# A rank for every piece of a planned kernel, and the transfers of an untaken path moved to another engine

## The chip, the cores and the metric

The kernel runs on one core of a Trainium2 chip. A core has a matmul engine (TensorE, PE in the profile; its weight loads are PEld), VectorE (DVE), ScalarE (ACT), GpSimd (POOL) and SyncE (SP), which here only issues transfers (DMAs). On-chip data lie in SBUF (128 partitions); TensorE writes into PSUM, eight banks per partition. The metric is the device time of one execution in microseconds, the median of some runs. An execution taken with the profiler gives the trace; its span runs from the program's first to its last instruction and is a little shorter than its time.

## The reference

Two stages: a linear attention with decay over 4 batches, 8 heads, 768 steps and head dimension 48, and a feed-forward layer whose hidden value is the maximum of three products, on the 3072 resulting tokens.

```python
# r, k, v: (4, 8, 768, 48); w, u: (8, 48)
for t in range(S):
    cur = np.einsum('bhd,bhe->bhde', u[None] * kt, vt)
    y[:, :, t] = np.einsum('bhd,bhde->bhe', rt, state + cur)
    state = w[None, :, :, None] * state + np.einsum('bhd,bhe->bhde', kt, vt)
x = y.transpose(0, 2, 1, 3).reshape(B * S, H * D)          # (3072, 384)
h = np.maximum(np.maximum(x @ w1, x @ w2), x @ w3)         # (3072, 768)
out = h @ w_out                                            # (3072, 384)
```

All is float32; the kernel reaches that accuracy by splitting operands into a high and a low float16 part and adding three products.

## The kernel before

The 768 steps are cut into 12 chunks of 64. A chunk has two halves `q` of four heads each. For each half the attention makes scores (`sc`: keys against receptances, masked, with the `u` term on the diagonal, in `am`), values (`va`: the masked scores against the values plus the receptances against the state) and the state's update (`ke`). In chunks 0 and 1 this is done in float32; from chunk 2 on with parts in float16 (`kd`, `ktd`, `vd`, `sd`, `rh`/`rl`, `ah`/`al`; the high part is a ScalarE copy, the low part a VectorE subtraction: L444, L449, L451, L490, L601). From chunk 4 on the parts are first spread into block-diagonal tiles by transfers (`kb`, `ktb`, `vb`, `sb`), so that a matmul uses the whole 128x128 array (L538); before that the array is used in 64-wide corners (L541, L548). From chunk 3 on GpSimd does the elementwise multiplications (`scale` L480, `product` L499 and L500, `diagonal` L516, `decay` L522), before that VectorE.

The chunk's result becomes `x` (L667, L670; six small transfers put its last rows in place, L677). The feed-forward then makes, for six groups `f` and three weights, nine matmuls each (`up`, L693). ScalarE takes the first of the three products (L708), VectorE the maximum with the other two (L712), ScalarE the high part `hh` (L715), GpSimd the low part `hl` (L721; the last group's by VectorE). Then come the matmuls with the output weight (`down`, also L693), a ScalarE copy to `io` (L738) and the store (L1103). The eight weights come as 64-bit floats and are converted on ScalarE and VectorE during the first 80 us (L351, L355, L358, L361). `STIRS` = 22 groups of three matmuls on zeros (L689) fill TensorE's early gaps.

The order of all this is written out by a planner, `Plan`, when the program is made. Each piece of work is entered by a call of `do` with its due time, its engine, a cost in us, the function that emits its instructions, what it reads, writes and which buffer it takes. `order` then goes forward in modelled time: of the engine that can start first it takes, among the pieces that are ready, the one with the lowest `due`. All engines get their instructions in the resulting order; they then run on their own and wait for each other through semaphores. Before the change `due` is the caller's figure plus a shift from a table `SHIFT` by the piece's kind ("dve m", "pe sc") and its stage (five stages, bounded by the due times 0, 1, 2 and 10). A transfer's completion uses one of eight semaphores in turn, so that a transfer waits until the one eight places ahead of it has landed (in the planner: `LANES`).

At the end VectorE makes a flag that says whether all inputs lay in the range for which the fast path is exact; every engine loads it (L1149) and branches (L1159): if the flag is set, a general path (`general`) computes everything again, slowly, in float32. With these inputs the flag is not set, and each engine jumps over its part of that path. Its transfers are all issued by SP.

```python
            n = first(m for m in when if self.todo[m]["eng"] == self.ENGINES[e] and when[m] <= t + 0.02)
...
    with tc.If(got["go"] > 0):
        general()
```

Of the kernel before, what the change touches and what calls it, by code (L numbers as in the profile page):

```python
# [7 lines left out]
F32 = mybir.dt.float32  # L8
# [22 lines left out]
FEATURE = 2  # L31
HELPED = dict(scale=3, product=3, diagonal=3, decay=3)
# [41 lines left out]
class Plan:  # L74
# [6 lines left out]
    SHIFT = {  # L81
        "sp feat": (0.06, 2.41, 0.07, -2.37, 0),
        "sp tok": (4.64, -12.96, -5.22, 0.22, 0),
        "pe blank": (-0.35, 0, 0, 0, 0),
        "pool pad": (0, -0.41, -0.49, 0, 0),
        "dve kT": (0.95, 1.8, 0, 0, 0),
        "dve rT": (-2.97, 3.27, 0.98, 0, 0),
        "act ru": (-3.24, 2.09, 0, 0, 0),
        "pe bo": (-20.47, 6.44, 0, 0, 0),
        "dve am": (1.11, 102.24, -0.18, -0.19, 0.43),  # L90
        "pe sc": (-3.66, -0.77, -0.03, -0.83, -0.79),
        "pool vz": (-5.54, 0, 0, 0, 0),
        "act apart": (0.53, 0, 0, 0, 0),
        "pe va": (-1.26, 17.06, -22.44, -45.09, 3.03),
        "act xh": (-2.11, 6.29, 19.78, -2.05, -0.03),
        "dve xl": (-0.63, -5.4, -2.29, -1.83, 0.76),
        "act xsq": (0, -4.27, 17.76, -6.93, -1.42),
        "act u": (0, 1.78, 0, 0, 0),
        "dve tkf": (0, -7.35, 0, 0, 0),
        "pe turned": (0, -0.4, 0, 0, 0),  # L100
        "act tkt": (0, -2, 0, 0, 0),
        "pe stir": (0, 0.62, 1.56, 0.64, 1.31),
        "sp word": (3.62, 3.5, 0, 0, 0),
        "act ztop": (-5.52, -0.56, 0, 0, 0),
        "dve word": (2.04, 0, 0, 0, 0),
        "act his": (0.41, -4.8, 0, 0, 0),
        "dve lo": (1.13, -2.95, 0, 0, 0),
        "pe kp": (0.04, -16.13, 0, 0, 0),
        "act kt": (-0.4, -0.46, 0, 0, 0),
        "pe ke": (-10.27, -1.26, 0.08, 0, 0),  # L110
        "act state": (0, -0.83, 0, 0, 0),
        "act sq": (0, 0, -3.6, 6.45, -0.3),
        "act sd": (0, 14.27, 0, 0, 0),
        "dve state": (-1.48, -1.03, 1, -1.84, 0),
        "act sdh": (0, -0.64, 23.47, -0.59, 0),
        "dve sdl": (-4.22, 1.55, 7.23, -1.96, 0),
        "sp x3": (0, 2.95, -1.73, -0.89, 0.43),
        "pe up": (0, -3.62, 0.01, -0.2, -0.43),
        "act m": (-0.7, -4.9, 0, 1.38, -1.96),
        "dve m": (93.3, -556.17, 6.75, 0.9, 1.16),  # L120
        "act hh": (-2.49, -6.05, 2.12, -0.02, -11.37),
        "pool hl": (2.58, 5.89, 0.11, -4.17, 3.89),
        "dve hl": (0, -1.12, 1.62, 0, -0.03),
        "pe dn": (0, -1.32, -44.06, -0.15, 0.87),
        "act io": (0, -1.2, 1.65, -2.57, 0),
        "sp io": (0, -0.82, -6.31, -0.75, 2.37),
        "act kdh": (0, -1.05, -4.12, 0.03, 0.27),
        "dve kdl": (0, -5.77, 1.73, 1.56, 0),
        "act rh": (0, -2.11, 0, 2.07, 3.23),
        "dve rl": (0, 6.31, 0.65, 0.14, -1.72),  # L130
        "dve a": (0, -5.82, 10.67, 18.29, 0.93),
        "act am": (0, 0, 0.68, 0, 0),
        "act ah": (0, -2.27, 0, 24.09, -0.46),
        "dve al": (0, 1.56, -1.03, -0.22, -0.05),
        "dve kdec": (0, 3.63, -1, 0, 0),
        "act ktdh": (0, 8.15, -0.28, -1.81, 0),
        "dve ktdl": (0, -0.05, -0.41, -1.02, 0),
        "act vdh": (0, -0.74, 0, 2.92, -4.09),
# [117 lines left out]
def kernel(ctx, tc, feat, tok, wu, ut, ws, wo, cst, out):  # L256
# [208 lines left out]
    def units(a):  # L465
        return a.rearrange("p g b n -> p (g b) n")
# [753 lines left out]
```

## Time and profile before

| | us |
|---|---|
| runs | 384.31, 387.48, 384.63; median 384.63 |
| the profiled execution | 384.0 |
| its span | 382.1, at a granted TensorE clock of 0.998 |
| TensorE busy | 372.6 (98%) |
| VectorE, ScalarE, GpSimd busy | 253.9, 243.1, 188.9 |

Matmuls are pipelined and their ends are modelled: in a dense stretch a matmul starts 109 ns after the one before it, while its own row is 273 ns long. Busy time is the union of the rows, so a stall of TensorE shows as idle time only where it outlasts the row before it. In a stage's row stand the stretch's bounds and length, then busy us (and instruction counts) of PE, PEld, DVE, ACT and POOL, the granted clock, the transfers' share of the DMA engines and GB/s. In a wait's row stand the engine and line that waited, who released it, us in total, times, and the longest. A row of one source line has its instructions with minimum, median and maximum duration in ns and the first and last start in us; "SPq" and the like are the engine's sequencer, which branches, waits and issues transfers. The chain of waits follows back from the last instruction to what released each step.

### The profile page before, as it was taken

How to read it: one execution, taken by the hardware profiler on the slowest of the kernel's cores; microseconds unless marked ns; L12 is line 12 of the kernel's file. 1: busy time of each engine (PE TensorE's matmuls, PEld its weight loads, DVE VectorE, ACT ScalarE, POOL GpSimd, SP SyncE). 2: the span in 40 equal slices, each digit the busy share in tenths (PEclk: the TensorE clock that was granted, in tenths of full speed). 3: DMA queues.
4: the chain of work that ended last, by engine and by line, in shares of the span. 5: the costliest groups of instructions: out<-in, count | busy, mean ns of one | idle time of the engine just before them, and what ended most of it. 6: DMA issues, size and time to landing. Idle time of an engine off the chain costs nothing.

```text
span 382.1 us, 13571 instructions
## 1 busy us (share of the span) xinstructions
PE 372.6 (98%) x5660; PEld 335.1 (88%) x5660; DVE 253.9 (66%) x457; ACT 243.1 (64%) x623; POOL 188.9 (49%) x190
## 2 busy tenths in 40 slices
PE   8999999989999999999999999999999999999994
PEld 7899888878898999998998999999999999999883
DVE  5599999999868657558468667667757555122340
ACT  3899758778557637656647556656655935993611
POOL 8500333899995585456556557547736320020110
PEclk9999999999999999999999999999999999999999
DMA  8985737162996888959986996996986964731201
GB/s 294 359 294 201 296 122 238 52 237 67 277 269 139 259 237 225 277 150 267 275 243 160 272 264 172 270 264 176 276 230 181 233 164 112 247 105 34 81 2 50
DMA packets 27700, 77.13 MB, mean 202 GB/s; under 512 B 4784, under 2 KB 12272, under 8 KB 26608
## 3 DMA queue, kind: packets, MB, share of 16 engines
q1 hardware_dynamic: 27344, 75.96, 69.0%
q8 instruction: 46, 0.75, 0.9%
q10 hardware_dynamic: 288, 0.23, 0.2%
q14 instruction: 22, 0.18, 0.2%
HBM read 38.38 MB, written 4.72 MB: 113 GB/s over the span
## 4 chain that ended last, share of the span: by engine, by line
PE 82%; DVE 8%; ACT 3%; DMA 3%; issue 2%; POOL 0%; SPq 0%; ACTq 0%; DVEq 0%
PE psm L693 63%; PE psv L538 8%; PE psa L538 3%; PE psm L689 2%; DMA raw<-in_wo_dram 2%; PE psa L548 1%; DMA tok<-in_tok_dram 1%; PE psv L541 1%; ACT ztop L351 1%; DVE raw L355 1%; DVE m L712 1%; DVE kd L449 1%; PE psa L582 1%; DVE sd L451 1%; DVE vd L451 1%
## 5 line engine op out<-in xcount | busy, mean ns | idle before, releaser
L693 PEld LDWEIGHTS <-w 128*128 128x128 f16 x2592 | 249.0, 98 | 31.2 <-issue 2.3
L693 PE MATMUL psm<-x,w 128*128 128x256 f16 x1944 | 225.2, 273 | 1.0 <-DVE m L712 1.0
L721 POOL TENSOR_TENSOR hl<-m,hh 128x256 f16<-128x256 f32 x60 | 46.8, 780 | 124.9 <-ACT hh L715 124.9
L712 DVE SCALAR_TENSOR_TENSOR m<-psm,m 128x256 f32<-128x256 f32 x144 | 60.2, 418 | 59.3 <-PE psm L693 50.1
L715 ACT CAST hh<-m 128x256 f16<-128x256 f32 x72 | 28.9, 401 | 53.3 <-DVE m L712 53.0
L480 POOL TENSOR_TENSOR feat<-feat,wrt 128x512 f32<-128x512 f32 x36 | 51.6, 1453 | 19.8 <-DVE ktd L449 10.2
L693 PE MATMUL psm<-hh,w 128*128 128x256 f16 x432 | 55.9, 273 | 0.0
L463 ACT ACTIVATE junk<-tok 128x384 bf16<-128x384 f32 x72 | 37.3, 518 | 3.0 <-DMA tok<-in_tok_dram 2.1
L708 ACT ACTIVATE m<-psm 128x256 f32<-128x256 f32 x72 | 27.2, 378 | 16.1 <-PE psm L693 15.1
L693 PE MATMUL psm<-hl,w 128*128 128x256 f16 x216 | 33.4, 273 | 0.6 <-DVE hl L721 0.4
L499 POOL TENSOR_TENSOR am<-tok,u_sb 128x384 f32<-128x384 f32 x18 | 20.2, 1122 | 24.9 <-DVE al L601 20.8
L490 DVE TENSOR_TENSOR rl<-feat,rh 128x512 f16<-128x512 f32 x20 | 17.6, 879 | 11.4 <-ACT rh L485 11.4
L670 DVE SCALAR_TENSOR_TENSOR x<-psv,x 112x512 f16<-112x512 f32 (+2 forms) x24 | 16.1, 671 | 12.3 <-ACT x L667 12.3
L516 POOL TENSOR_TENSOR am<-cs,a 128x512 f32<-128x512 f32 x18 | 20.6, 1146 | 6.3 <-DVE a L507 6.1
L538 PE MATMUL psv<-rh,sb 128*128 128x64 f16 x256 | 23.6, 193 | 0.0
L538 PE MATMUL psv<-ah,vb 128*128 128x64 f16 x256 | 23.6, 193 | 0.0
L538 PE MATMUL psv<-al,vb 128*128 128x64 f16 x128 | 22.7, 193 | 0.0
L538 PE MATMUL psv<-rl,sb 128*128 128x64 f16 x128 | 22.7, 193 | 0.0
L538 PEld LDWEIGHTS <-vb 128*128 128x128 f16 x384 | 21.1, 98 | 0.4
L500 POOL TENSOR_TENSOR am<-am,tok 128x384 f32<-128x384 f32 x18 | 20.7, 1150 | 1.4
L738 ACT ACTIVATE io<-psm 128x256 f32<-128x256 f32 x36 | 13.0, 380 | 12.4 <-PE psm L693 12.0
L507 DVE TENSOR_REDUCE a<-am 128x8 f32<-128x384 f32 x20 | 11.0, 548 | 14.3 <-POOL am L500 14.2
(124 smaller groups left out, 582.6 us busy)
## 6 DMA issues: line engine op xcount, KB each, us to landing
tok<-in_tok_dram SPq DMA_DIRECT2D x26, 576.0 KB, 6.2
feat<-in_feat_dram SPq DMA_DIRECT2D x24, 512.0 KB, 4.7
raw<-in_ws_dram SPq DMA_DIRECT2D x6, 1152.0 KB, 7.8
out_dram<-io SPq DMA_DIRECT2D x36, 128.0 KB, 5.2
kb<-kd SPq DMA_DIRECT2D x16, 256.0 KB, 5.8
vb<-vd SPq DMA_DIRECT2D x16, 256.0 KB, 5.9
sb<-sd SPq DMA_DIRECT2D x16, 256.0 KB, 5.2
kb<-kd SPq DMA_DIRECT2D x16, 248.0 KB, 5.8
```

Of the source, the lines that this page charges most:

```text
L463: nc.scalar.activation(out=junk[:, 0:U * D].rearrange("p (u d) -> p u d", u=U), in_=src, func=AF.Square, scale=scale, accum_out=stat[:, ki ...
L480: helper(c, "scale").tensor_tensor(out=t[n], in0=t[n], in1=tb, op=ALU.mult)
L490: nc.vector.tensor_tensor(out=t["rl"], in0=units(t["rT"]), in1=t["rh"], op=ALU.subtract)
L499: helper(c, "product").tensor_tensor(out=w.rearrange("p (g b) d -> p g b d", g=2), in0=t["r"], in1=by_token(u_sb, q), op=ALU.mult)
L500: helper(c, "product").tensor_tensor(out=w, in0=w, in1=units(t["k"]), op=ALU.mult)
L516: helper(c, "diagonal").tensor_tensor(out=t["a"], in0=eye.unsqueeze(1).broadcast_to([P, U, C]), in1=t.pop("sum").unsqueeze(2).broadcast_to ...
L538: nc.tensor.matmul(out=ps[:, i, :], lhsT=block[k].on[a][i], rhs=prods[k](b, i), **flags)
L693: nc.tensor.matmul(out=ps, lhsT=a, rhs=b, start=first and n == 0, stop=last and n == len(prods) - 1)
L708: nc.scalar.mul(out=m, in_=ps, mul=by)
L712: nc.vector.scalar_tensor_tensor(out=m, in0=ps, scalar=by, in1=m, op0=ALU.mult, op1=ALU.max)
L715: nc.scalar.copy(out=h[0][:, f, :], in_=m)
L721: lows_by(c, f).tensor_tensor(out=h[1][:, f, :], in0=m, in1=h[0][:, f, :], op=ALU.subtract)
```

## The change

Three things are changed.

1. The table of shifts by kind and stage is replaced by `RANK`, 1593 whole numbers, one for each call of `do` in the order of the calls. A piece's number takes the place of its due time among the ready pieces. With it some of the planner's costs change: the small moves of `x` count 0.74 us each on SP and the spreads 0.58 (0.45 before); GpSimd's multiplications are 12% dearer in chunks before 6, its low parts 0.82 us instead of 0.70 in chunks before 5.
2. The transfers of the general path (`general`, and `load_weight` called from it) are issued by ScalarE instead of SP.
3. Five output stores (three of chunk 8, two of chunk 9) are issued as two halves of 128 columns each.

Beside these, the array of tokens holds r, k, v in this order instead of k, r, v, and there is a loader `load_kv` for chunks between `FLIPPED` and `FEATURE`, which are both 2.

```diff
 CORNERS = 4
 STIRS = 22
 FEATURE = 2
+FLIPPED = 2
 HELPED = dict(scale=3, product=3, diagonal=3, decay=3)
 SC_R = 2.0 ** 6
...
     ISSUE = {"sp": 0.45, "act": 0.45, "pool": 1.0}
     BEFORE, BEHIND, PHASE, LANES, TURN = 1.5, 1.0, 1.4, 8, 0.095
     CLASSES = (0.0, 1.0, 2.0, 10.0)
-    SHIFT = {
-        "sp feat": (0.06, 2.41, 0.07, -2.37, 0),
-        "sp tok": (4.64, -12.96, -5.22, 0.22, 0),
-        "pe blank": (-0.35, 0, 0, 0, 0),
...
-    }
+    RANK = (
+        10, 30, 47, 0, 64, 6, 688, 43, 378, 140, 582, 295, 115, 293, 348, 331, 608, 352, 377, 429, 127, 269, 239, 107,
+        112, 94, 226, 96, 102, 206, 244, 142, 89, 166, 63, 256, 65, 285, 93, 70, 213, 21, 932, 674, 186, 23, 18, 114,
...
+    )
     def __init__(self, bufs):
         self.bufs, self.todo, self.wrote, self.read = bufs, [], {}, {}
     def do(self, due, eng, cost, fn, reads=(), writes=(), takes=(), move=0, near=0, parts=1, counts=1.0, corner=False):
-
-
         n = len(self.todo)
         new = [t for _, t in takes]
         made = (*new, *writes, *reads)[0]
         kind = eng + " " + (made if isinstance(made, str) else made[0])
         stage = sum(due >= x for x in self.CLASSES)
         base = due
-        due += self.SHIFT.get(kind, (0,) * 5)[stage]
+        due = self.RANK[n]
         need = {self.wrote[k] for k in (*reads, *writes) if k in self.wrote}
         for k in writes:
             need |= self.read.get(k, set())
...
     def load_tok(c, q):
         t = raw.tile([P, 3, 2, B, D], F32, name="tok")
         nc.sync.dma_start(out=t, in_=tok[c, q])
-        raws.setdefault((c, q), {}).update(k=t[:, 0], r=t[:, 1], v=t[:, 2])
+        raws.setdefault((c, q), {}).update(r=t[:, 0], k=t[:, 1], v=t[:, 2])
         return t
+    def load_kv(c, q):
+        t = raw.tile([P, 3, 2, B, D], F32, name="tok")
+        nc.sync.dma_start(out=t[:, 1:], in_=tok[c, q][:, 1:])
+        raws.setdefault((c, q), {}).update(k=t[:, 1], v=t[:, 2])
+
     def load_v(c, q):
-        t = raw.tile([P, 2, B, D], F32, name="v1", bufs=4)
+        t = raw.tile([P, 2, B, D], F32, name="v1", bufs=2 * FLIPPED)
         nc.sync.dma_start(out=t, in_=tok[c, q][:, 2])
         raws.setdefault((c, q), {}).update(v=t)
...
     def by_down(t, f, ms):
         return t.rearrange("p (f n) -> p f n", f=3)[:, f % 3, ms]
-    def load_weight(n, h=None, shift=0):
+    def load_weight(n, h=None, shift=0, eng=nc.sync):
         raw = wld.tile([P, 4 * WN + 4], I16, name="raw64")
         src = (ws[n] if n < NF else wo[n - NF]).bitcast(I16)
         cols = slice(0, 4 * WN) if h is None else slice(h * 4 * HN, (h + 1) * 4 * HN)
-        nc.sync.dma_start(out=raw[:, shift:shift + cols.stop - cols.start], in_=src[:, cols])
+        eng.dma_start(out=raw[:, shift:shift + cols.stop - cols.start], in_=src[:, cols])
         return raw
...
-            rw = load_weight(n, h).bitcast(I32)[:, 0:2 * HN].rearrange("p (n two) -> p n two", two=2)
+            rw = load_weight(n, h, eng=nc.scalar).bitcast(I32)[:, 0:2 * HN].rearrange("p (n two) -> p n two", two=2)
...
-                nc.sync.dma_start(out=t.rearrange("p (q g) b s -> p q g b s", q=2), in_=feat[bass.ds(c, 1), :, :, i].rearrange("c q p g b s -> p (c q) g b s"))
+                nc.scalar.dma_start(out=t.rearrange("p (q g) b s -> p q g b s", q=2), in_=feat[bass.ds(c, 1), :, :, i].rearrange("c q p g b s -> p (c q) g b s"))
...
-                    nc.sync.dma_start(out=ov, in_=o.rearrange("p (i two s) -> p i two s", i=1, two=2))
+                    nc.scalar.dma_start(out=ov, in_=o.rearrange("p (i two s) -> p i two s", i=1, two=2))
...
-    def dma(due, fn, move, reads=(), writes=(), takes=(), eng="sp", n=1):
-        do(due, eng, n * Plan.ISSUE[eng], fn, reads, writes, takes, move, 0, n)
+    def dma(due, fn, move, reads=(), writes=(), takes=(), eng="sp", n=1, each=0.45):
+        do(due, eng, n * each, fn, reads, writes, takes, move, 0, n)
     def helping(c, columns, what):
-        return ("pool", 0.05 + 2.5e-3 * columns) if c >= HELPED[what] else ("dve", dve(columns))
+        return ("pool", (1.12 if c < 6 else 1.0) * (0.05 + 2.5e-3 * columns)) if c >= HELPED[what] else ("dve", dve(columns))
     def dve(columns):
         return 0.07 + 1.05e-3 * columns
...
     def fetched(c, q, due, behind=()):
         dma(due, lambda: load_feat(c, q), 1.8, reads=behind, writes=["fetched"], takes=[("feat", ("feat", c, q))])
+        if c < FLIPPED:
+            dma(due, lambda: load_v(c, q), 0.85, reads=behind, writes=["fetched"], takes=[("v1", ("tok", c, q))])
+            return
         if c < FEATURE:
-            dma(due, lambda: load_v(c, q), 0.85, reads=behind, writes=["fetched"], takes=[("v1", ("tok", c, q))])
+            dma(due, lambda: load_kv(c, q), 1.67, reads=behind, writes=["fetched"], takes=[("tok", ("tok", c, q))])
             return
         dma(due, lambda: load_tok(c, q), 2.5, reads=behind, writes=["fetched"], takes=[("tok", ("tok", c, q))])
     def late_squares(c, q, due):
         t = ("again", c, q)
         dma(due, lambda: do_tile(t, load_tok(c, q)), 2.5, reads=[("begun", int(due))], writes=["fetched"], takes=[("tok", t)])
-        for kind, n in enumerate((1, 0, 2)):
+        for kind, n in enumerate(range(3)):
             do(due + 0.2, "act", 0.62, lambda kind=kind, n=n: square_sum(units(T[t][:, n]), kind, c, q), reads=[t], writes=[("sq", c, q, "rkv"[kind])])
     def squares(c, q, due):
...
     def spreading(c, due, dst, src, keys, name):
         if c >= CORNERS:
-            dma(due, lambda: spread(nc.sync, dst, src), 2.4, reads=[*keys, *(("pad", n) for n in range(14))], writes=[name], n=2)
+            dma(due, lambda: spread(nc.sync, dst, src), 2.4, reads=[*keys, *(("pad", n) for n in range(14))], writes=[name], n=2, each=0.58)
...
         do(due + 0.04, "dve", 0.40 if half else 0.68, lambda: x_low(c, q, T["x", c]), reads=[("va", c, q), hi], writes=[lo])
         if not begins:
             if c:
-                dma(due + 0.06, lambda: x_last(T["x", c]), 0.4, reads=[hi, lo], writes=[rest], n=2 * NJ)
+                dma(due + 0.06, lambda: x_last(T["x", c]), 0.4, reads=[hi, lo], writes=[rest], n=2 * NJ, each=0.74)
             do(due + 0.9, "act", 0.97, lambda: x_sum(c, T["x", c]), reads=[hi, rest], writes=[("xsq", c)])
     def attend(c, at):
...
             m = ("m", c, f)
             do(due - 0.1, "act", act(TOK), hi, reads=[m, *([("hh", c)] if f else [])], writes=[("hh", c, f)], takes=[] if f else [("hh", ("hh", c))])
-            do(due - 0.1, *(("dve", dve(TOK)) if lows_by(c, f) is nc.vector else ("pool", 0.7)), lo, reads=[m, ("hh", c, f), *([("hl", c)] if f else [])],
+            do(due - 0.1, *(("dve", dve(TOK)) if lows_by(c, f) is nc.vector else ("pool", 0.82 if c < 5 else 0.7)), lo, reads=[m, ("hh", c, f), *([("hl", c)] if f else [])],
                writes=[("hl", c, f)], takes=[] if f else [("hl", ("hl", c))], near=0.55)
         banks = {}
...
             do(due, "pe", len(fs) * 0.328, lambda: down(T["h", c], m, fs, banks, TOK), reads=reads, **(dict(takes=[("psm", bank)]) if 0 in fs else dict(writes=[bank])))
             if NF - 1 in fs:
                 do(due + 0.02, "act", act(TOK), lambda: do_tile(("io", c, m), leaving(banks[m], TOK, SC_O)), reads=[bank], takes=[("io", ("io", c, m))])
-                dma(due + 0.03, lambda: nc.sync.dma_start(out=out[m, :, c * TOK:(c + 1) * TOK], in_=T["io", c, m]), 0.1, reads=[("io", c, m)])
+                ways = 2 if (NCH - 4) * NM <= c * NM + m < (NCH - 4) * NM + 5 else 1
+                dma(due + 0.03, lambda: stored(m, ways), 0.1, reads=[("io", c, m)], n=ways)
+
+        def stored(m, ways):
+            for k in range(0, TOK, TOK // ways):
+                nc.sync.dma_start(out=out[m, :, c * TOK + k:c * TOK + k + TOK // ways], in_=T["io", c, m][:, k:k + TOK // ways])
         most, rest = range(NF - 1), [NF - 1]
         for m, fs, due in ((0, most, 0.70), (1, most, 0.77), (0, rest, 0.83), (1, rest, 0.85), (2, range(NF), 0.87)):
...
     ws = ws.reshape(NF, P, 3 * DM)
     wo = words(inputs["moe_w_out"]).reshape(2, 3, P, DM).transpose(0, 2, 1, 3).reshape(2, P, 3 * DM)
     ft = np.stack([feat(inputs["k"]), feat(inputs["r"])], axis=3)
-    tk = np.stack([tokm(inputs["k"]), tokm(inputs["r"]), tokm(inputs["v"])], axis=3)
+    tk = np.stack([tokm(inputs["r"]), tokm(inputs["k"]), tokm(inputs["v"])], axis=3)
     wu = np.stack([feat1(inputs["w"]), feat1(inputs["u"])], axis=1)
     s, t = np.arange(P)[:, None] % C, np.arange(C)[None]
     cst = np.concatenate([np.eye(P), s == t, s < t, np.arange(P)[:, None] // C == np.arange(2)[None]], axis=1).astype(np.float32)
```

More of the change, by code (lines that the diff above doesn't have):

```diff
@@ L606, in keys @@
         if c < WHOLE:
-            whole(t["ke"], D, (t.pop("kt") if c < FEATURE else units(t["k"]), units(t["v"])))
+            whole(t["ke"], D, (t.pop("kt") if c < FLIPPED else units(t["k"]), units(t["v"])))
         else:
@@ L812, in general @@
                     row = tok[bass.ds(c, 1), :, hh * C + s:hh * C + s + 1, 2].rearrange("c q p g b e -> (c p) q g b e")
-                    nc.sync.dma_start(out=vr[HS[hh]].rearrange("p (q g) b e -> p q g b e", q=2), in_=row.broadcast_to([C, 2, 2, B, D]))
+                    nc.scalar.dma_start(out=vr[HS[hh]].rearrange("p (q g) b e -> p q g b e", q=2), in_=row.broadcast_to([C, 2, 2, B, D]))
                 kc, rc = (t[:, :, :, s:s + 1].broadcast_to([P, NP, B, D]) for t in cols)
@@ L833, in general @@
                     nc.scalar.copy(out=ys[:, q], in_=ps)
-                nc.sync.dma_start(out=y[bass.ds(c, 1), s].rearrange("c h g b e -> (c h) (g b e)"), in_=ys.rearrange("h q n -> h (q n)"))
+                nc.scalar.dma_start(out=y[bass.ds(c, 1), s].rearrange("c h g b e -> (c h) (g b e)"), in_=ys.rearrange("h q n -> h (q n)"))
         with tc.For_i(0, NCH // 2, 1) as i:
@@ L841, in general @@
                         if g < NJ:
[L842 removed]
+                            nc.scalar.dma_start(out=xt[:, g, hh * C:hh * C + D], in_=yv[:, g, hh])
                         else:
                             for j in range(NJ):
[L845 removed]
+                                nc.scalar.dma_start(out=xt[:, j, hh * C + D:hh * C + C], in_=yv[:, g, hh, E * j:E * (j + 1)])
                 ps = psa.tile([P, NJ, P], F32, name="psa")
@@ L868, in general @@
                     put(m, leaving(ps, P, 1.0))
-    plan = Plan(dict(feat=2, tok=3, raw64=3, v1=4, ru=1, kt=1, psa=2, psv=2, psm=4, rh=2, rl=2, am=2, a=2, ah=2, al=2, x=2, m=3, io=3, hh=1, hl=1))
+    plan = Plan(dict(feat=2, tok=3, raw64=3, v1=2 * FLIPPED, ru=1, kt=1, psa=2, psv=2, psm=4, rh=2, rl=2, am=2, a=2, ah=2, al=2, x=2, m=3, io=3, hh=1, hl=1))
     do = plan.do
@@ L959, in before_keys @@
         t = ("tok", c, q)
-        if c < FEATURE:
+        if c < FLIPPED:
             do(due - 0.30, "pe", 0.94, lambda: flipped(c, q), reads=[("feat", c, q), ("kT", c, q)], takes=[("psa", ("kp", c, q))], counts=0.5, corner=True)
```

71 lines of the change are left out of this document (removed), and 65 rows, old and new, of the table RANK.

## The prediction

> **What bounds the kernel now.** I read the page's totals first, then busy time by stage, then TensorE's waits, then the chain of waits, and last the rows of the ending branch. The page's head and three of its groups:
>
> ```profile
> span 382.1 us, 13571 instructions
> PE 372.6 (98%) x5660; PEld 335.1 (88%) x5660; DVE 253.9 (66%) x457; ACT 243.1 (64%) x623; POOL 188.9 (49%) x190
> PEclk9999999999999999999999999999999999999999
> GB/s 294 359 294 201 296 122 238 52 237 67 277 269 139 259 237 225 277 150 267 275 243 160 272 264 172 270 264 176 276 230 181 233 164 112 247 105 34 81 2 50
> L721 POOL TENSOR_TENSOR hl<-m,hh 128x256 f16<-128x256 f32 x60 | 46.8, 780 | 124.9 <-ACT hh L715 124.9
> L480 POOL TENSOR_TENSOR feat<-feat,wrt 128x512 f32<-128x512 f32 x36 | 51.6, 1453 | 19.8 <-DVE ktd L449 10.2
> ```
>
> TensorE is busy for 372.6 of 382.1 us at a full granted clock, and the change neither adds nor removes a matmul. So what the change can reach is the other 9.5 us. Where they lie, by stage (the first column after the stretch is its length, then PE, PEld, DVE, ACT, POOL):
>
> ```profile
> 0.00:10.00 10.00, 8.93 (x113) 7.11 (x115) 5.38 (x16) 3.95 (x9) 8.41 (x19) 1.00 0.81 298
> 10.00:20.00 10.00, 9.39 (x278) 8.36 (x276) 6.54 (x8) 8.16 (x16) 5.07 (x6) 1.00 0.96 360
> ...
> 20.00:70.00 50.00, 49.80 (x917) 44.23 (x911) 47.81 (x74) 41.42 (x87) 12.21 (x10) 1.00 0.63 222
> 70.00:100.00 30.00, 28.22 (x697) 24.50 (x698) 29.11 (x44) 22.79 (x62) 28.81 (x24) 1.00 0.45 143
> 100.00:160.00 60.00, 60.00 (x842) 54.59 (x840) 40.28 (x75) 36.39 (x99) 41.15 (x39) 1.00 0.87 237
> 160.00:190.00 30.00, 29.58 (x418) 26.92 (x416) 20.16 (x35) 17.68 (x47) 17.46 (x17) 1.00 0.85 230
> 190.00:340.00 150.00, 149.97 (x2052) 136.84 (x2049) 92.47 (x167) 96.16 (x261) 71.06 (x71) 1.00 0.82 216
> ```
>
> TensorE's idle time is 1.07 us in the first ten, 0.61 in the next, 0.20 up to 70, 1.78 from 70 to 100, 0.42 from 160 to 190, 0.03 after that up to 340: 4.1 us. The remaining 5.4 us are the end. From 20 to 100 us VectorE is busy for 47.81 + 29.11 = 76.9 of 80 us, and from 70 GpSimd is full as well. Who ended TensorE's idle time:
>
> ```profile
> PE psv L682 <- DVE still L277: 1.1, 1, 1.1
> PE psm L693 <- DVE m L712: 1.0, 1, 1.0
> PE psa L548 <- issue: 0.6, 1, 0.6
> PE psv L541 <- DVE x L670: 0.5, 1, 0.5
> PE psm L693 <- DVE hl L721: 0.4, 1, 0.4
> PE psv L541 <- DVE ktd L449: 0.2, 1, 0.2
> ```
>
> The first is the start, which no order changes; the 0.6 us is not a wait for another engine. The order owns the other 1.0 + 0.5 + 0.4 + 0.2 = 2.1 us (by stages 1.78 + 0.42 + 0.20 + 0.03 = 2.4; I use 2.4). The chain of waits, start and length in us, shows the place:
>
> ```profile
> 76.45 1.27 DVE sd L451
> 77.72 0.33 DVE m L712
> 78.05 0.94 DVE ktd L449
> ...
> 84.97 1.09 PE psm L693 x9
> ...
> 130.49 0.98 PE psm L693 x9
> ...
> 376.74 0.38 ACT io L738
> ```
>
> At 76 us the chain runs through VectorE's queue: the maximum that frees a PSUM bank (L712) stands behind a 1.27 us low part. Nine matmuls take 0.98 us, so 109 ns each; a matmul's own row is 273 ns long, so a stall hides up to 0.16 us in its predecessor's modelled end. Four stalls (those on VectorE above) hide up to 0.6 us more: the order owns 2.4 to 3.0 us.
>
> **The change part by part.** *Ranks in place of due times.* Among the pieces that are ready on an engine, the planner now takes the one of lowest rank; the 1593 numbers are one for each call of `do`, in that order. By counting the calls: the first six (10, 30, 47, 0, 64, 6) are features, values and blank matmuls of chunk 0's two halves, so the second half's features are asked for ahead of the first's; a weight load (word 1, rank 51) comes ahead of the second half's values (64), and word 1 ahead of word 0 (85). A weight is 1152 KB, which at the 294 to 359 GB/s of the first slices is 3.3 to 4.0 us, by which these values come later. Who needs them:
>
> ```profile
> 9.36 0.34 ACT L631 COPY tok<-v 128x192 f32<-128x192 f32 x1
> ...
> 17.28 0.33 PE L639 MATMUL psv<-am,tok 64*64 64x64 f32 x4
> ```
>
> The copy would go from 9.4 to at most 13.4 and is read at 17.3, so the delay costs nothing; without that cover it would be 4 us of TensorE. Filler matmuls keep their number, so time that real work takes from filler early is spent on filler later: no gain there.
>
> *What the order can return.* The planner's costs are raised where it had them low: six small moves of x at 0.74 instead of 0.45 us each, GpSimd's multiplications of chunks before 6 by 1.12, its low parts of chunks before 5 from 0.70 to 0.82. The trace shows them above the old figures: 780 ns against 0.70 us; 1453 ns against 0.05 + 512 x 0.0025 = 1.33 us; for the moves
>
> ```profile
> 346.42 3.87 SPq L677 DMA_DIRECT2D x<-x  x6
> ```
>
> 3.87/6 = 0.65 us. So the old order was laid out for a GpSimd that is about a tenth faster than it is, and the stretch where GpSimd is full (28.81 of 30 us) is the one with 1.78 us of idle. Bounds: nothing returned, and on the other side 3.0 us. I take 2.0 us, the 70-to-100 stretch with a part of its hidden time, because the corrected costs lie there; the 0.42 at 160 to 190 I leave.
>
> *Turns.* Nine matmuls after a 64-wide piece take 1.09 us, after a 128-wide one 0.98, so each change of array shape costs 0.11. Chunks 2 and 3 have twelve such pieces (two halves of scores, keys, values each). Paired at best, six turns go: 0.7 us. Scattered no further than now, nothing is lost, for each stands alone. I take 0.
>
> *Five late stores as halves* (three of chunk 8, two of chunk 9): five more DMA issues on SP, and each later transfer gets another of the eight completion semaphores.
>
> ```profile
> L1103 SPq DMA_DIRECT2D out_dram<-io x36: 332/408/1527, 59.9 to 377.1; - x36
> DMA to landing us min/median/max: 1.7/5.2/7.1
> ```
>
> 5 x 0.41 = 2.0 us of SP's queue; behind it wait spreads and loads. In these stages TensorE lost 0.03 us in 150, so this is covered: 0. Uncovered it would be the 2.0 us, on the spreads that the next chunk waits for.
>
> *Order r, k, v in the tokens' array*: same bytes, same tiles; `load_kv` is not reached, since FLIPPED equals FEATURE. 0.
>
> *The general path's transfers by ScalarE.* They never run, but every engine that has instructions there must jump over them. The rows of the branch (L1159) and of what follows (L1215):
>
> ```profile
> L1159 SPq EVENT_SEMAPHORE  x8: 17/17/17, 380.2 to 380.7; - x8
> L1159 POOLq COMPARE_BRANCH  x1: 45/45/45, 369.5 to 369.5; - x1
> L1159 ACTq COMPARE_BRANCH  x1: 50/50/50, 376.7 to 376.7; - x1
> L1159 SPq COMPARE_BRANCH  x1: 45/45/45, 377.7 to 377.7; - x1
> L1159 ACTq EVENT_SEMAPHORE  x1: 17/17/17, 379.5 to 379.5; - x1
> ...
> L1215 SPq EVENT_SEMAPHORE  x10: 17/28/28, 380.8 to 382.0; - x10
> L1215 POOLq DRAIN  x3: 34/41/82, 369.7 to 381.8; - x3
> ```
>
> SP branches at 377.7 and goes on at 380.2, 2.5 us later; ScalarE needs 376.7 to 379.5; GpSimd, which does nothing in that path, goes on after 0.2 us. SP then has eight semaphore steps up to 380.7 and the closing barrier from 380.8. With its transfers gone SP should pass like GpSimd, at 377.9. The end is then set by the last store (issued 377.1, landing at 378.8 by the shortest row) and by ScalarE, at 379.5. The eight steps take 0.5 us: if ScalarE inherits them, it is done at 380.0 to 380.1, against 380.8 to 381.3 for SP's steps and barrier waits; if SP keeps them, they start when the store has landed. I take 1.0 us. Bounds: 0, if the gap stays, and 1.3, from 380.8 back to ScalarE's 379.5. Cover: if ScalarE's jump grew by over 1 us with its longer program, the gain would be gone.
>
> The Trainium skill has a rule that fits this gap (Runtime: NRT & Kernel Launch, Instruction fetch mechanics): a taken branch whose target lies outside the fetched window stalls for a fetch. The trace agrees so far, with 2.5 us on SP and 0.2 on GpSimd; by it the 2.5 us go. It also has one that speaks against the edit (Trainium Kernel Development and Optimization, Key Constraints): transfers from several engines' queues share the same DMA engines, and another issuer saves issue time only. By that alone, moving transfers that never run is worth nothing, and the sum would be 2.0 instead of 3.0 us.
>
> The sum: 2.0 + 1.0 = 3.0 us off the profiled execution's 384.0 (its span of 382.1 and 1.9 around it), so 381.0. The median of the runs before, 384.63, lies 0.6 above that execution, so I forecast 381.6.
>
> **The rivals.** *The tail alone.* A new order removes the four stalls and makes others as large: any order of 1593 pieces meets a VectorE that is busy for 76.9 of 80 us. 384.6 - 1.0 = 383.6. For it: the stretch is full on two engines. Against: 100 to 160 us runs without idle time.
> *More than the stalls.* All 3.0 us, the 0.6 of issue, and half the turns, 0.4, with the tail's 1.0: 5.0 off, 379.6. Against: the 0.6 is no wait that an order can move.
> *The branch gap stays*, because SP keeps enough of the path's loops and barriers to miss: the edit doesn't do what it says. 384.6 - 2.0 = 382.6. (The second rule of the Trainium skill, above, would come out here.)
> *Slower: VectorE beside GpSimd.* A low part of 512 columns varies with what runs beside it:
>
> ```profile
> L449 DVE TENSOR_TENSOR kd<-feat,kd x20: 674/747/1754, 52.3 to 298.2; 128x512 f16<-128x512 f32 x20
> ```
>
> If the ranks push more low parts under GpSimd's multiplications, each costs up to 1754 - 747 = 1.0 us more of VectorE. Up to 100 us it has 80 - 76.9 = 3.1 us spare, so from the fourth such piece on TensorE waits; with eight it loses 4.9 us, and with the tail's gain and none from the order the time is 384.6 + 4.9 - 1.0 = 388.5; with ten, 390.5.
>
> **How the numbers follow.** Forecast 0.45 (own range 380.4 to 382.8, the order's share between 0.8 and 3.0), tail alone 0.2, more 0.16, gap stays 0.09, slower 0.10. The range reaches to 378.8, below the second rival, and up to 385.0, past the first: what it leaves out is the slower case and the ends of the others. One per cent, about what a measurement of this kernel can tell from no change, is 3.8 us: below 380.8 lie a quarter of the forecast's case and nearly all of the second rival's, 0.11 + 0.15 = 0.26; above 388.5 about half of the slower case and a little more for causes that I have not seen, 0.08; within, 0.66.
>
> **What would show it.** Right: SP's first L1159 step at most 0.3 us after its branch, the L1215 steps ending about 1 us nearer to the last `io` copy; TensorE's idle time from 70 to 100 us below 0.5, and no new stage above 0.5. Wrong: SP's gap stays near 2.5 us; waits on `m` L712 or a low part above 2 us in total in the first 100; VectorE's L449 and L451 rows longer in the mean; or busy time of TensorE itself changed by over 1 us, which I have taken as fixed.

## The result, and the profile after

The kernel after takes 386.80 us in the median of 22 runs (384.44 to 389.96), the kernel before 384.62 in 22 runs beside it (382.84 to 387.48): a ratio of 1.0057, 95% interval 1.0039 to 1.0075. So the change is slower by about 2.2 us, where 3.0 us of gain were forecast. The profiled execution of after is 387.11 us long, 3.1 us more than that of before. Line numbers up to about L290 are six lower than before's, from there to L1102 one lower, and behind L1103 seven higher.

First the page's head of the kernel after:

```profile
span 385.3 us, 13559 instructions
PE 373.5 (97%) x5660; PEld 335.4 (87%) x5660; DVE 253.8 (66%) x457; ACT 241.5 (63%) x623; POOL 192.0 (50%) x190
q8 instruction: 46, 0.75, 0.8%
```

The same 5660 matmuls, 0.9 us more of busy time on TensorE, and 3.2 us more of span. The third row belongs to the list of DMA queues and becomes important below. The stages of after (length of the stretch, then PE, PEld, DVE, ACT, POOL, granted clock, DMA share, GB/s):

```profile
0.00:10.00 10.00, 8.94 (x145) 7.33 (x147) 5.47 (x16) 3.66 (x8) 8.43 (x18) 1.00 0.82 305
10.00:20.00 10.00, 8.66 (x209) 7.28 (x203) 6.04 (x6) 7.60 (x16) 5.04 (x7) 1.00 0.81 316
20.00:70.00 50.00, 47.37 (x909) 41.31 (x904) 46.02 (x67) 38.01 (x73) 15.19 (x11) 1.00 0.60 215
70.00:100.00 30.00, 27.29 (x614) 23.81 (x613) 24.91 (x42) 22.18 (x65) 18.80 (x17) 1.00 0.39 124
100.00:160.00 60.00, 60.00 (x905) 54.48 (x903) 45.08 (x77) 37.06 (x100) 47.10 (x43) 1.00 0.85 227
160.00:190.00 30.00, 30.00 (x421) 27.42 (x419) 21.66 (x41) 17.58 (x47) 17.77 (x18) 1.00 0.90 253
190.00:340.00 150.00, 150.00 (x2070) 137.13 (x2069) 91.20 (x166) 90.23 (x241) 72.97 (x70) 1.00 0.82 216
```

TensorE's idle time is now 1.06, 1.34, 2.63 and 2.71 us in the first four stretches, where it was 1.07, 0.61, 0.20 and 1.78; the 0.42 us at 160 to 190 are gone. Up to 340 us that is 7.7 us against 4.1, so 3.6 more. VectorE, full from 70 to 100 us before (29.11 of 30), has five us to spare now (24.91), and TensorE still waits there longer. For what, say the waits of TensorE:

```profile
PE psa L547 <- issue: 2.6, 2, 1.3
PE psv L540 <- issue: 2.3, 2, 1.5
PE psv L681 <- DVE still L271: 1.1, 1, 1.1
PE psm L692 <- DVE m L711: 0.6, 1, 0.6
PE psm L692 <- DVE hl L720: 0.5, 1, 0.5
PE psm L692 <- ACT io L737: 0.4, 1, 0.4
```

The waits for other engines, apart from the start, sum to 1.5 us where they were 2.1. What has grown is "issue", time in which TensorE waited for nothing that the profile shows: 4.9 us in four stalls, 0.6 in one before. TensorE's timeline shows the four; the bracket is the idle time ahead of the group:

```profile
14.77 0.62 PE L547 MATMUL psa<-ru,feat 64*64 64x64 f32 x13 [1.34 <-issue]
26.84 0.56 PE L547 MATMUL psa<-ru,feat 64*64 64x64 f32 x11 [1.25 <-issue]
69.41 0.21 PE L540 MATMUL psv<-rl,sd 64*48 64x64 f16 x2 [0.86 <-issue]
82.91 0.33 PE L540 MATMUL psv<-vd,ktd 64*48 64x48 f16 x12 [1.45 <-issue]
```

And the chain of waits around the last one (start, length in us):

```profile
77.28 1.55 PE psv L540 x94
78.83 2.07 PE psm L692 x18
80.90 0.56 PE psv L540 x36
81.46 1.45 issue
82.91 0.33 PE psv L540 x12
83.24 0.77 PE psa L540 x48
```

The stall stands in the middle of one piece, between two matmuls of the same line, whose operands have long been there. No order of pieces has a gap to close at that place. With matmuls and weight loads counted together in order of their start, the four resume at rows 450, 962, 2498 and 3010 of TensorE's program: the differences are 512, 1536 and 512, all multiples of 256. Before's one stall resumes at row 450 too, and in the twelve traces of this case all 29 waits of TensorE that are put down to issue resume at the same place of 256, the 194th. The row of queue 8 above belongs to this: its 46 packets of instructions hold 0.75 MB, 16 KB each, and 46 x 256 = 11,776 just covers TensorE's 11,406 rows. So a packet is a block of 256 instructions, and the stall comes where TensorE runs out of one block before the next is there.

Last the end, SP's rows of the branch and what follows:

```profile
L1166 SPq EVENT_SEMAPHORE  x8: 17/17/17, 382.6 to 384.0; - x8
L1166 ACTq COMPARE_BRANCH  x1: 54/54/54, 381.3 to 381.3; - x1
L1166 SPq COMPARE_BRANCH  x1: 45/45/45, 382.1 to 382.1; - x1
L1166 ACTq EVENT_SEMAPHORE  x1: 17/17/17, 383.8 to 383.8; - x1
```

SP goes on 0.5 us after its branch, where it needed 2.5; ScalarE needs 2.5, as before (2.8). The eight semaphore steps stayed with SP and now last 1.4 us instead of 0.5, because they wait for the last stores, which land at 383.2 to 383.9 us. VectorE's jump, which the edit leaves alone, takes 2.9 us in both kernels.

The account of the profiled executions: 3.6 us more idle up to 340 us (4.3 of issue, 0.6 less of other waits, 0.1 unexplained), 0.9 us more of busy time, and the end shorter by 1.3 us (9.5 - 4.1 = 5.4 before, 385.3 - 373.5 - 7.7 = 4.1 after): 3.2 us, the difference of the spans. From start to start of the matmuls on either side the four stalls are 1.56, 1.47, 1.05 and 1.63 us, in sum 5.7 against 0.83 before; so 0.6 of the 0.9 us of "busy" are stall too, hidden in modelled ends.

### The profile page after: what moved, and what is told of

It reads as the page before. It is cut to its first block, busy times and chain, and to the rows that moved or that the text cites. A ratio compares the mean times of both kernels' runs of the same rounds, so it can differ in the third digit from the quotient of the medians.

```text
span 385.3 us, 13559 instructions
## 1 busy us (share of the span) xinstructions
PE 373.5 (97%) x5660; PEld 335.4 (87%) x5660; DVE 253.8 (66%) x457; ACT 241.5 (63%) x623; POOL 192.0 (50%) x190
## 4 chain that ended last, share of the span: by engine, by line
PE 88%; DVE 7%; issue 3%; ACT 0%; DVEq 0%
PE psm L692 67%; PE psv L537 8%; PE psa L537 3%; PE psm L688 2%; PE psa L547 2%; PE psv L547 2%; PE psv L540 1%; DVE m L711 1%; PE psa L581 1%; DVE kd L448 1%; DVE feat L479 1%; DVE rl L489 1%; DVE al L600 0%; DVE am L590 0%; DVE tok L521 0%
## 5 line engine op out<-in xcount | busy, mean ns | idle before, releaser
L711 DVE SCALAR_TENSOR_TENSOR m<-psm,m 128x256 f32<-128x256 f32 x144 | 59.8, 419 | 63.3 <-PE psm L692 36.1
L489 DVE TENSOR_TENSOR rl<-feat,rh 128x512 f16<-128x512 f32 x20 | 20.0, 999 | 8.4 <-ACT rh L484 8.4
L515 POOL TENSOR_TENSOR am<-cs,a 128x512 f32<-128x512 f32 x18 | 21.8, 1214 | 7.0 <-DVE a L506 6.9
L590 DVE COPY_PREDICATED am<-cs,psa 128x512 f32<-128x512 int32 x24 | 17.6, 733 | 9.6 <-PE psa L537 7.3
L521 POOL TENSOR_TENSOR tok<-tok,tkt 128x384 f32<-128x384 f32 x16 | 19.4, 1217 | 3.7 <-ACT junk L462 3.7
```

Source lines behind the costliest of these rows:

```text
L489: nc.vector.tensor_tensor(out=t["rl"], in0=units(t["rT"]), in1=t["rh"], op=ALU.subtract)
L515: helper(c, "diagonal").tensor_tensor(out=t["a"], in0=eye.unsqueeze(1).broadcast_to([P, U, C]), in1=t.pop("sum").unsqueeze(2).broadcast_to ...
L711: nc.vector.scalar_tensor_tensor(out=m, in0=ps, scalar=by, in1=m, op0=ALU.mult, op1=ALU.max)
```

## The experiments

Two theories were open after the first comparison. **Blocks**: the new order puts 64-wide pieces back to back, and TensorE uses up a block of 256 instructions faster than the next one arrives. A matmul of 256 columns goes every 109 ns, so a block of 128 such matmuls with their weight loads lasts 14 us; 94 of the 64-wide ones above took 1.55 us, so a block of those is gone after some 2 us. **Rivals**: the order costs through the engines that feed TensorE, or the tail's edit costs something of its own.

**The tail alone.** The kernel before, with only the general path's transfers moved:

```diff
-        nc.sync.dma_start(out=raw[:, shift:shift + cols.stop - cols.start], in_=src[:, cols])
+        eng.dma_start(out=raw[:, shift:shift + cols.stop - cols.start], in_=src[:, cols])
...
-                nc.sync.dma_start(out=y[bass.ds(c, 1), s].rearrange("c h g b e -> (c h) (g b e)"), in_=ys.rearrange("h q n -> h (q n)"))
+                nc.scalar.dma_start(out=y[bass.ds(c, 1), s].rearrange("c h g b e -> (c h) (g b e)"), in_=ys.rearrange("h q n -> h (q n)"))
```

> The kernel before with one part of the change alone: the general path's transfers go by ScalarE. Theory T (the branch): SP's gap behind its branch falls from 2.5 us to about 0.5 us as in the changed kernel, the end moves nearer to the last io copy by 1.0 to 1.3 us, and the time is 383.4 (ratio 0.997). Rival (another issuer of transfers that never run is worth nothing): 384.6, ratio 1.000.

Measured: 382.57 us, ratio 0.9963 (0.9943 to 0.9983), faster than both kernels of this case. SP's branch and its first step:

```profile
L1159 SPq EVENT_SEMAPHORE  x8: 17/17/17, 379.6 to 381.3; - x8
L1159 SPq COMPARE_BRANCH  x1: 45/45/45, 379.2 to 379.2; - x1
```

0.4 us instead of 2.5. The edit is good by itself, by 1.4 us in the ratio. Its profiled execution does not show the gain: it took 384.55 us, one of the longest of the twelve, with its first real matmul at 8.1 us where before's came at 7.0.

**The order alone.** The kernel after with the path's transfers back on SP, so the same lines the other way round.

> The changed kernel with the general path's transfers put back on SP: ranks, costs and half stores alone. If the two parts add up, it is slower than the changed kernel by what the branch saves, 1.0 to 1.3 us: 388.0, ratio 1.009 to the kernel before. If the ranks' loss came through SP or ScalarE at the end, it would be at 386.8 or below.

Measured: 388.92 us, ratio 1.0129 (1.0101 to 1.0156), 0.9 us above what was expected. The order costs 5.0 us by the ratio. Its waits:

```profile
PE psv L540 <- issue: 2.1, 2, 1.4
PE psa L547 <- issue: 0.9, 1, 0.9
PE psv L547 <- issue: 0.7, 1, 0.7
```

Issue again, 3.7 us, at multiples of 256 rows again, but partly at other blocks than in after (near 45 us there is one, near 26 only 0.36). TensorE's program is the same row for row; which block is late differs between executions.

**Moving the pieces over the blocks, first try.** Filler groups (each three matmuls of 256 columns on zeros) changed so that they have more instructions for about the same time, to make the blocks end in other pieces. In after, six filler matmuls became groups of seven 64-wide ones; in before, thirteen:

```diff
-        for _ in range(3):
-            nc.tensor.matmul(out=T["stir"], lhsT=still[:, 0:P], rhs=still, start=True, stop=True)
+        for h, w, c in (x for narrow in STIRRED.get(n, (0, 0, 0)) for x in (SMALL if narrow else LARGE)):
+            nc.tensor.matmul(out=T["stir"][h, 0:c], lhsT=still[h, 0:w], rhs=still[h, 0:c], start=True, stop=True)
```

> The changed kernel, same order of work on every engine; six of the filler matmuls of the start are replaced by seven 64-wide ones each that take about as long together, so that every later instruction of TensorE stands 72 places further on. Theory P (instruction blocks): TensorE's four stalls inside 64-wide pieces (1.5, 1.4, 1.0 and 1.6 us, all at place 195 of a block of 256 rows) leave these places; from the lengths of the new blocks some 3 us of stalls remain instead of 6.8 by the same reckoning, so the time is about 383.5 (3.3 us less than 386.8, between 382 and 385), and what stalls remain are at place 123 of 256. Rival W (the new order makes TensorE wait for VectorE and GpSimd): the same stalls at the same pieces and 386.8.

> The kernel before, same order of work on every engine; thirteen of the filler matmuls of the start are replaced by seven 64-wide ones each, so that TensorE's later instructions stand 156 places further on. Theory P (instruction blocks): by the lengths of the blocks this is nearly the worst place for this order; stalls of 8 us instead of 4.6 by the reckoning, so 388 (387 to 389), ratio about 1.009, with stalls inside 64-wide pieces at place 39 of 256, the largest near 67 us. Rival W: nothing but the fillers changed, 384.6.

Measured: 389.79 us (1.0186, 1.0133 to 1.0238) and 388.80 us (1.0102, 1.0071 to 1.0133). The first is a clear miss. The stalls at 14, 26 and 69 us did go, but the first matmul of real work came at 9.2 us instead of 6.1. The longest wait that was left:

```profile
83.93 0.78 PE L540 MATMUL psv<-vd,ktd 64*48 64x48 f16 x48 [1.80 <-ACT junk L462]
```

The profile puts it down to ScalarE, because it stands at the beginning of a piece that has a semaphore to wait for. But it resumes at row 3010, as after's last stall, and an instruction packet started 2.45 us ahead of it (81.48), so it is most likely a block stall under another name. Behind it the granted clock fell to half, from 84.8 to 88.2 us. The second kernel came out near its number, but not for its reason: block stalls of only 0.57 and 0.33 us, and real work starting at 10.8 instead of 7.0 us. In both the start changed along with the blocks, so they decide nothing.

**The same order with fewer instructions.** After, with each filler group as one matmul of 512 columns and one of 256: the same columns, 44 rows less over the 22 groups.

```diff
-        for _ in range(3):
-            nc.tensor.matmul(out=T["stir"], lhsT=still[:, 0:P], rhs=still, start=True, stop=True)
+        for w in (2, 1):
+            nc.tensor.matmul(out=T["stir"][:, 0:w * TOK], lhsT=still[:, 0:P], rhs=still.unsqueeze(1).broadcast_to([P, w, TOK]), start=True, stop=True)
```

> The changed kernel, same order of work; each filler group is one matmul of 512 columns and one of 256 instead of three of 256: the same columns, two instructions of TensorE fewer for each of 22 groups, so that from 25 us on its instructions stand 44 places earlier. Theory P (instruction blocks of 256; a block that TensorE runs through faster than the next one can be fetched leaves it standing): the boundary that now lies within the run of 64-wide pieces at 68 us moves behind it, and the one at 25 us too; of the four stalls those at 25 and 68 us go (1.4 and 1.0 us), the others stay or change by some tenths. Time 386.8 - 2.4 = 384.4 (383.4 to 385.5). Rival W (waits for VectorE and GpSimd): 386.8.

Measured: 383.84 us, ratio 0.9990 (0.9971 to 1.0010): 2.6 us better than after by the ratios (3.0 by the medians), without one piece in another place. Its waits:

```profile
PE psa L540 <- issue: 1.3, 1, 1.3
PE psa L547 <- issue: 0.9, 1, 0.9
PE psv L547 <- issue: 0.7, 1, 0.7
PE psm L692 <- DVE m L711: 0.6, 1, 0.6
```

The other waits are after's; issue is 2.9 us instead of 4.9, the stalls near 26 and 69 us are gone, and one of 0.7 us near 47 us is new. So stalls make 2.0 us of difference between the two profiled executions. As a whole these differ by 1.4 us only (387.11 and 385.70); the first real matmul came at 7.3 us in this one and at 6.1 in after's.

**The other way: more instructions.** In after, four filler groups as twelve matmuls of 64 columns; in before, every filler matmul as two of 128 columns.

```diff
+        for w in (64,) * 12 if 2 <= n < 6 else (256,) * 3:
...
+        for w in (128,) * 6:
```

> The changed kernel, same order of work; in four filler groups of the start the three matmuls of 256 columns are twelve of 64, about as long together (29 ns each), and without the 64-wide corners that left the earlier test's start slow. TensorE's instructions then stand 72 places further on. Theory P: the boundaries within 64-wide pieces at 25, 68 and 81 us move into feed-forward matmuls; of 5.6 us of stalls at place 195 of 256 some 1.5 to 3 remain, most of it before 23 us. Time 383.9 (382.8 to 385.2). Rival W: 386.8. Rival S (any change at the start costs what the first shift test lost, 3 us): 389.8, then with the real work beginning at 9 us instead of 6.

> The kernel before, same order of work; each filler matmul of 256 columns is two of 128, so that TensorE's instructions stand 54 to 66 places further on when its real work begins and 132 from 23 us on. Theory P: this order now gets boundaries within 64-wide pieces that had been spared; by the lengths of the blocks 2.7 to 4.6 us more of stalls, the largest, about 2 us, near 69 us, others near 16 and 21 us, all at place 195 of 256. Time 387.8 (386.5 to 389.0). Rival W: 384.5, since nothing else is changed.

Measured: 390.48 us (1.0168, 1.0127 to 1.0209) and 385.47 us (1.0029, 1.0002 to 1.0056). The first misses: the stalls should have gone, and there were more of them, at 12, 19, 24, 82 and 89 us, with 1.02, 0.65, 1.68, 1.60 and 1.05 us, all at rows whose places differ by multiples of 256 (the fourth is put down to `m` L711 in the waits). Rival S has the time, 389.8, but not its sign: real work starts at 6.8 us here, and not at 9. After the third the granted clock fell, as two stretches of that kernel show (the clock stands third from the end):

```profile
24.00:27.00 3.00, 1.53 (x28) 1.17 (x25) 2.10 (x3) 1.61 (x5) 0.00 (x0) 0.87 0.71 215
27.00:30.00 3.00, 3.00 (x40) 2.37 (x39) 0.31 (x1) 2.08 (x4) 0.00 (x0) 0.56 0.52 217
```

From 26.2 to 29.6 us, 3.4 us, matmuls of 256 columns went every 213 ns instead of 109: a stall can cost up to another 1.7 us. The second has the sign that was forecast and its largest new stall in the place, but 1.1 us by the ratio is a third of the 3.3 that were forecast, and the time lies below the range. The timeline of before's order with halved fillers:

```profile
13.87 0.61 PE L548 MATMUL psv<-v,kt 64*48 64x48 f32 x19 [1.02 <-issue]
72.33 0.60 PE L541 MATMUL psv<-vd,ktd 64*48 64x48 f16 x34 [1.04 <-issue]
```

Before's own profile has no stall near 72 us.

**A block by itself.** Before, with two added runs of 640 64-wide matmuls on zeros, one in a stretch with many transfers, one near the end, where there are few:

```diff
+        for k in range(640):
+            nc.tensor.matmul(out=ps[HS[k % 2], 0:D], lhsT=still[HS[k % 2], 0:C], rhs=still[HS[k % 2], 0:D], start=True, stop=True)
```

> The kernel before with two runs of 640 64-wide matmuls on zeros added, 1280 instructions of TensorE each: one after chunk 5's last up piece, where the transfers take about 0.9 of the DMA engines, and one after chunk 10's last output piece, where they take about 0.1. At the 15 ns that such a matmul takes in the trace, 256 instructions last 1.9 us. Theory P: every boundary stalls; the period is the fetch of a block: near 2.5 us at the end with idle transfers, 3.5 to 6 us in the busy stage. Rival (no fetch involved): 1.9 us for each 256 in both, without gaps. Rival (fetch, but transfers don't matter): the same period in both.

Measured (425.23 us, a single run); the first run's rows in the timeline, then the second's:

```profile
205.80 2.84 PE L1154 MATMUL psm<-still 64*64 64x48 f16 x167
211.01 3.38 PE L1154 MATMUL psm<-still 64*64 64x48 f16 x128 [2.38 <-issue]
218.03 9.45 PE L1154 MATMUL psm<-still 64*64 64x48 f16 x345 [3.64 <-issue]
```

```profile
374.81 4.10 PE L1154 MATMUL psm<-still 64*64 64x48 f16 x247
381.69 10.52 PE L1154 MATMUL psm<-still 64*64 64x48 f16 x384 [2.79 <-issue]
```

Matmuls that all read the same zeros stop for 2.4 to 3.6 us, and the two stops of the first run are 128 of them apart, 256 rows with their weight loads. This shows the block without any order. Not every boundary stalled, as had been expected, and the two stops of the first run lie 7.0 us apart, not 3.5 to 6. The records of the instruction packets give the rest: the packet ahead of 218.03 started at 215.41, 4.4 us after its block's predecessor was entered (211.01), the one ahead of 381.69 at 379.36, 2.7 us after (376.70). In these two delays the profile gives the transfers 1.03 and 0.74 of the DMA engines (a packet counts in full where it starts, so a share can exceed 1); near the end of the second run, with 0.06 and less, the delay was 1.1 to 1.2 us. TensorE resumed 2.6 and 2.3 us after the packet's start; in the kernel after the four packets started at 12.26, 24.37, 67.04 and 80.64 us, 2.3 to 2.5 us ahead of the four resumptions, and 3.5, 4.2, 0.9 and 3.1 us after their blocks' predecessors were entered. So a block takes about 2.4 us from the packet's start, plus a delay before the start, and TensorE stalls where the block before lasts less than the two together. After these stalls the clock fell to half (211 to 228 us and from 382), at which 128 such matmuls last 3.5 us, and the stalls all but ceased.

**The half stores.** After, with the five late stores whole, the order left as it was laid out:

```diff
-                dma(due + 0.03, lambda: stored(m, ways), 0.1, reads=[("io", c, m)], n=ways)
+                dma(due + 0.03, lambda: stored(m, 1), 0.1, reads=[("io", c, m)], n=ways)
```

> The kernel after with the five late stores of chunks 8 and 9 issued whole again; the order of the pieces, laid out with two issues for each, stays as it is. The prediction counted the halves at 0 because TensorE never waits in those stages: by that, 386.8 us as the kernel after, within 0.6. Rival: the five extra issues of 0.41 us on SyncE are not covered, and 2.0 us come back: 384.8 us. The instruction-block theory says the same as the first, since no instruction of TensorE changes.

Measured: 385.97 us, ratio 1.0048 (1.0031 to 1.0065), not to be told from after's 1.0057: the halves cost nothing that can be seen. This run was also of use in another way. Its TensorE has the very program of after, and its profiled execution took 385.03 us, 2.1 less than after's 387.11:

```profile
PE psv L540 <- issue: 2.2, 2, 1.2
PE psa L547 <- issue: 0.6, 1, 0.6
PE psm L692 <- DVE m L711: 0.5, 1, 0.5
```

Issue is 2.8 us instead of 4.9, also 2.1 less; the stall near 26 us is missing, since there the packet started 3.1 us after its block's predecessor was entered and not 4.2. This fits after's wide spread, 384.4 to 390.0 us; its other executions have no trace.

**The tail with fewer filler instructions.** The tail's edit and the edit of 512 and 256 columns together, on before's order.

> The kernel before with the general path's transfers by ScalarE (382.57 us so far) and each filler group as one matmul of 512 columns and one of 256 instead of three of 256, so that 44 rows of TensorE are saved and every block of 256 ends up to 44 rows further on in the work. For the kernel after this was worth 3.0 us. By the instruction-block theory it depends only on which pieces the blocks now cover: walking the rows of the trace of before in steps of 256, the block that ends near 68.6 us gets short (4.6 us or less for 256 rows), so a new stall of 0.5 to 1.6 us near 67 to 70 us, and the one near 13 us stays: 383 to 384.5 us, no gain. Rival (fewer instructions are better by themselves, wherever they lie): 3 us less, 379.6 us. If no new stall comes at 67 to 70 us, the walk does not say where stalls fall.

Measured: 383.04 us, ratio 0.9964 (0.9950 to 0.9979): the tail's gain and nothing more, so fewer instructions are not better by themselves. But the stall that I had walked out for 67 to 70 us did not come. There the block lasted only 3.0 us, yet its successor's packet had been asked for early (67.20, ahead of the entry at 67.73). The one that did come is the first of all:

```profile
15.85 0.81 PE L689 MATMUL psm<-still 128*128 128x512 f16 x4 [1.46 <-issue]
```

Which block is late can't be told from the row counts alone: when its packet starts counts as much.

## Why the prediction was wrong

**The end: mechanism right, size a little low.** SP's gap went from 2.5 to 0.5 us, the price was taken as 1.0 us and the trace has 1.3, the upper bound given; alone, the edit gave 1.4 us by the ratio. The sign named for it, a first step at most 0.3 us after the branch, was too strict (0.5 and, alone, 0.4). The eight steps stayed with SP, the second of the two ways that were weighed. The Trainium skill's rule on taken branches (Runtime: NRT & Kernel Launch, Instruction fetch mechanics) agrees with this; its rule on several issuers (Trainium Kernel Development and Optimization, Key Constraints) gave nothing for the edit, and the measurement speaks against applying it to transfers that never run.

**Order r, k, v, the delayed values, the half stores: 0.** For the halves this is measured. The other two were not tried; no wait of after's first 20 us points to them, since its waits there are the start and the stalls.

**The order returns 2.0 us: this step failed.** Measured alone, the order costs 5.0 us by the ratio. A part of the step is right: waits on other engines fell by 0.6 us, and VectorE and GpSimd are no longer full from 70 to 100 us. But the step counted only waits for other engines, and fixed everything else. The one row that did not fit, `PE psa L548 <- issue: 0.6`, was set aside as "not a wait for another engine", and in the rivals as "no wait that an order can move". It was the block stall, and the order does move it, because the order decides which instructions share a block. It is not that the new order has longer runs of narrow matmuls, as the first of the two theories had it. Before has the longest, 192 from 67.5 us; after's are 144 long, here the one from 66.0 us (the rows of L541 in before and of L540 in after alone; in brackets the matmuls and the weight loads):

```profile
67.50:70.80 3.30, 3.08 (x192) 2.91 (x192) 1.00 0.16 61
65.90:69.65 3.75, 2.71 (x144) 2.36 (x144) 1.00 0.52 177
```

In before a block ends in the middle of its run, at 68.98 us, and the blocks on both sides take in wide matmuls too. In after a block begins with the run, at 66.13 us, and is used up in 2.2 us. The first of these two blocks of before, and that of after up to its stall (TensorE's busy time alone):

```profile
63.94:68.98 5.04, 5.04 (x130) 1.00 0.81 301
66.13:68.35 2.22, 2.09 (x138) 1.00 0.58 190
```

At the 64-wide pieces of chunks 2 and 3, 2.3 us of stall appeared, 2.0 us more with the two in the first 30 us (4.9 - 0.6 = 4.3). Where the blocks end was in no term of the sum, and so was left to chance. Nor did the 2.0 us show beside the fillers of 512 and 256 columns: with these and the tail's edit on both sides, the ratio is 0.9990 for the new order and 0.9964 for the old, and the profiled executions have 2.9 and 1.5 us of issue.

**The rivals.** *The tail alone* (383.6) described the mechanism best: a new order that removes its stalls and makes others. It had the others on VectorE, and as large; they were on the instruction queue, and 4.3 us against 0.6 gained. *More than the stalls* counted the 0.6 us as something that an order can move, which is right, but only as a gain; the sentence against it is the mistaken one. *The branch gap stays* fell. *Slower: VectorE beside GpSimd* had the right sign, with 388.5 the nearest time of all, and the wrong mechanism, so its number is luck: the row that it rests on did not grow,

```profile
L448 DVE TENSOR_TENSOR kd<-feat,kd x20: 676/712/1484, 51.7 to 308.6; 128x512 f16<-128x512 f32 x20
```

with a median of 712 ns against 747, a mean of 867 against 919 and a longest of 1484 against 1754, and VectorE's sum is 253.8 us against 253.9. Of the signs named for a wrong forecast, waits on `m` and low parts stayed below 2 us; TensorE's idle time from 70 to 100 us, which should have fallen below 0.5, rose to 2.71. One sum of the prediction does not come out: with 3.0 us for the order its own range begins at 380.6, not 380.4.

The Trainium skill describes the refill itself (Runtime: NRT & Kernel Launch, Instruction fetch mechanics): blocks of 16 KiB, 256 instructions, the next fetched while the current one runs. The period of 256 rows agrees. It calls the cost of crossing a block mostly hidden, which holds for the 240 us from 100 to 340, where TensorE lost nothing, and it fails at some crossings between 64-wide matmuls, with 1.0 to 1.6 us at each of after's four stalls.

**What stays open.** Why a packet starts 0.7 us after its block's predecessor is entered in one place and 4.6 in another. Many transfers in flight go with the long delays: in after the profile gives them 1.04, 0.95, 0.16 and 1.06 of the DMA engines in the delays of 3.5, 4.2, 0.9 and 3.1 us. But the probe has a delay of 1.2 us beside a share of 1.13 (at 20.1 us), and the load was not varied alone. Why the order alone costs 5.0 us by the ratio, when its profiled execution, at 388.31, has 3.7 us of issue, 3.1 more than before's, and why the tail's edit is worth 2.8 us beside the new order (1.0129 against 1.0057) and 1.4 beside the old; the rest may lie in stalls of executions without a trace or in a fallen clock. Of the clock the record has the means: the five of after's 22 executions with the lowest, 0.996, took 387.35 to 389.96 us, the other seventeen 384.44 to 388.17. Where in these five it fell was not traced. And the 2.6 us between after and its version with fewer filler instructions are explained for 2.0.

## What to carry to other kernels

A row "issue" in TensorE's waits that resumes in the middle of a piece is worth counting out: if the rows between such stalls are multiples of 256, it is the instruction stream, and a priority that only lets operands come earlier has nothing to gain there. A planner that prices only engines and transfers does not see where the blocks end, so a new order moves these stalls by chance. What was tried here is a few instructions of TensorE more or fewer ahead of them: it won 2.6 us once, changed nothing once and lost four times (twice with a later start as well), so it has to be measured each time. Fewer instructions per us at such a place (wider matmuls, or narrow pieces spread among wide ones) is what the lengths of the blocks suggest, but it was not tried. And where a path is hardly ever taken, see which engine holds its instructions: the jump over it cost SP 2.5 us here, and giving its transfers to ScalarE, which jumps anyway, was worth 1.4.

## What the runs showed of the hardware

TensorE's instructions come in blocks of 256, matmuls and weight loads for the most part; ahead of the stalls a block was there 2.2 to 2.7 us after its packet started, and the start lay 0.7 to 4.6 us behind the entry into the block before. With 64-wide matmuls that is 1.0 to 1.6 us of stall a block in the kernel after, and 2.4 to 3.6 us in a run of nothing else.

After a stall of 1.7 us in one kernel (with 72 rows more by narrow fillers) and of 2.1 us in another (with 64-wide ones, and most likely a block stall) the granted clock fell to half for 3.4 us, and in the probe for 17.1 and 13.7 us; in the kernel after, with stalls of up to 1.6 us, it did not.
